# Seven PSUM banks in one list for scores, maxima and all else, and the last sums by products with ones, in a clustered attention with a mixture of experts

## The chip, the core and the metric

One core of one Trainium2 chip runs the whole program. The metric is the device time of one execution in microseconds (us); the time shown for a kernel is the median of its runs. Names of the engines as in the profile: PE is TensorE (PEld its weight loads), DVE is VectorE, ACT is ScalarE, POOL is GpSimd, SP is the engine that issues most of the DMA (SPq in the profile).

## What is computed

A clustered attention, whose output feeds a mixture of experts. Queries and keys are each given to the nearest of 16 centroids of their head, a query sees only the keys of its own cluster, and the rest is softmax attention. The output, 3072 rows of 512, is the input x of the second half: rows with a positive skip score go to one of 8 experts.

```python
# batch, heads, seq, head_dim = 4, 8, 768, 64; 16 clusters
mask = q_assign[:, :, :, None] == k_assign[:, :, None, :]
scores = np.where(mask, scale * np.matmul(q, k.transpose(0, 1, 3, 2)), -1000000000.0)
attn = np.exp(scores - np.max(scores, axis=-1, keepdims=True))
attn = attn / (np.sum(attn, axis=-1, keepdims=True) + 1e-09)
x = attn @ v                                   # 3072 rows of 512
...
e_idx = np.argmax(xc @ w_gate, axis=1)         # for rows with x @ w_skip > 0
h = np.maximum(xc[mask] @ w1[e], 0.0)          # 512 -> 1024, 8 experts
y[mask] = gate_w[mask, None] * (h @ w2[e])     # 1024 -> 512
out[do_compute] = xc + y
```

## The kernel before

**The attention, pair by pair.** The four batches of eight heads make 16 pairs of heads (`npair`; HP = 4 pairs per batch). Scores are kept transposed, keys by queries: one score tile is 128 keys by 384 queries (HALF) of one head. A pair has NS = 24 of them: two halves of the queries (hf), six key tiles (kt), two heads (a). What each step does:

- `smax` (L549, L551): one product of 128 queries by 384 keys, and DVE's maximum over it, 24 per pair. They run for the next pair while the scores of this one run. `mneg` (L557) and `mrows` (L565, L570) turn the maxima into rows that are appended to the operand of the scores.
- `score` (L583, L584, L586): two products into one PSUM bank, and ACT's exp out of it into `PT`, a ring of 12 tiles in SBUF. POOL adds the tiles of the six key tiles up to one sum per half and head (L591, L597); for head 1 of the last pair DVE does.
- `avs` (L608): a group of products of `PT` with v, into the one bank "av", after every third key tile. `oT` keeps its result.
- `sums` (L644, L647), `recip` (L655), `turn_out` (L696) and `xout` with `scale_out` (L701, L718): the row sums by products with ones, their reciprocals, and the output turned and scaled.
- For the pairs to come: `load`, `sims` (L467, L474) and `assign` (L498, with `first_max` behind it) for the clusters, `masks` (L510, L514), and `split_hi` (ACT, L408), `split_lo` (L419, DVE), `copies_hi` (L426) and `copies_lo` (L432), which split q and k in a part of higher and one of lower precision and bring the parts to the operands by DMA on SP. The part of higher precision is kept in `HI[t]` (t = 0 for q, 1 for k), one buffer each for all pairs.

**The order of the work.** Nothing is scheduled by a tool across these steps: `steps` (L297) keeps all of them in a heap by due time and writes instructions in that order. One unit of time is one score; a pair's times count from its first score. The table `PLAN` holds the due times, `FIRST` other ones for the pairs 0, 1 and 2 (each step of them that is not named there takes its time from `PLAN`). A step that yields comes back to the heap at a later time. Every engine takes its instructions strictly in the order in which they were written.

**PSUM.** [...] Before, there are four pools: "ps" with two buffers for the scores, "sm0" to "sm2" for the maxima, "av" with one for the products with v, and "x_ps" with two for all else (clusters, masks, maxima rows, sums, turned outputs, routing). The buffers of a name are used in turn.

**The last pair and the first expert.** `ending` lists what is done with the last pair: sums of its two halves (`sums_last`, L667) and logits, routing of its rows (`gate` with L860 to L877, `route_c`, `route_d` with L922 and L927, `route_e`), and beside it the first expert's work on rows that are known already: `early_first`, `early_turn` and `early_second` take expert 0 through one layer, transposes and the second layer for 128 rows, `second_first` begins the first layer for the next 128 rows (its first half of the hidden columns, 12 products on PE at L986 to L988). `experts` then does the second half of that first layer, the transposes (`turn`, with L996 on PE, L998 on ACT and L999 on DVE), the second layer, and after it the other experts. Weights are read in pieces and split into two parts by ACT (L1229) and DVE (L1230).

Of the kernel before, what the change touches and what calls it, by code (L numbers as in the profile page):

```python
# [12 lines left out]
F32 = mybir.dt.float32  # L13
# [27 lines left out]
NPS = (2, 3, 1, 2)  # L41
# [28 lines left out]
        "load": -62.0, "load_v": -37.0, "assign": (-34.6, 0.25, 0.02, 6.0, 0.02, 0.02), "masks": (-26.0, 0.12), "smax": (-17.6, 0.97, 0.0), "mneg": (-6.4, 5.2),  # L70
# [6 lines left out]
class Kernel:  # L77
# [113 lines left out]
    def attention(self, ctx):  # L191
# [8 lines left out]
        self.st, self.nsm = {}, count()  # L200
# [11 lines left out]
    def centroids(self, cn):  # L212
# [16 lines left out]
        cps = self.xps([P, P])  # L229
# [3 lines left out]
        for t in range(2):  # L233
# [5 lines left out]
            self.cb.append(c)  # L239

# [24 lines left out]
    def keep_busy(self, n, w=4):  # L265

        if not hasattr(self, "idle"):
            self.idle = self.ps_av.tile([P, 512], F32, name="av")
# [101 lines left out]
    def bank(self, name):  # L370
        return (self.ps_st if name == "ps" else self.ps_sm).tile([P, 512], F32, name=name)

    def xps(self, shape):
        return self.ps_x.tile(shape, F32, name="x_ps", tag="x_ps")
# [85 lines left out]
    def sims(self, i):  # L460

        c, nc = self.st[i], self.nc
        sp = self.xps([P, HALF])
# [12 lines left out]
    def first_max(self, vals, n, w, out, tag, pool, wait):  # L476
# [6 lines left out]
        nc.vector.tensor_tensor(out=eq, in0=vals, in1=mx.unsqueeze(2).to_broadcast([P, n, w]), op=ALU.is_ge)  # L483
        yield next(wait)
# [9 lines left out]
    def assign(self, i, *wait):  # L494
        c, nc = self.st[i], self.nc
        tp = self.xps([P, NB, P])
# [6 lines left out]
        yield from self.first_max(tp.rearrange("p b (g c) -> p (b g) c", c=NCL), NB * 8, NCL, oh, "c", self.small, wait)  # L503

    def masks(self, i, wait):

        c, nc = self.st[i], self.nc
        mp = self.xps([P, HALF])
# [5 lines left out]
        nc.scalar.activation(out=mk, in_=mp, func=AF.Identity, scale=self.mscale, bias=self.mbias)  # L514
        yield 0.3
# [19 lines left out]
    def masks_first(self, i):  # L535

        mp = {}
        for t, hf in ((1, 0), (0, 0), (1, 1), (0, 1)):
            mp[t, hf] = self.xps([P, HALF]) if hf == 0 else self.bank("ps")[:, :HALF]
            self.mask_rows(i, t, hf, mp[t, hf])  # L540
        for t, hf, a in ((1, 0, 0), (0, 0, 0), (1, 1, 0), (1, 0, 1), (0, 0, 1), (1, 1, 1), (0, 1, 0), (0, 1, 1)):
            self.mask_out(i, t, hf, a, mp[t, hf])

    def smax(self, i, n):
# [3 lines left out]
        sm = self.bank(f"sm{next(self.nsm) % 3}")[:, :HALF]  # L548
# [896 lines left out]
```

## Time and profile before

| | |
|---|---|
| median of 3 runs | 692.94 us (692.67 to 693.31) |
| the profiled execution's own time | 692.28 us |
| its span, first to last instruction | 690.2 us |
| mean granted clock of TensorE | 0.994 |
| PE / DVE / ACT / POOL busy | 666.2 / 502.4 / 418.4 / 357.7 us |
| DMA | 110.17 MB in 54354 packets, mean 160 GB/s |

The attention fills the span to about 480 us, one pair every 28 us from about 40 us on; the experts follow. In the profile a row of a group names line, engine, operation, the tile that is written and those that are read, the count, the busy time with the mean of one in ns, and the idle time before it with what ended that. "x_ps", "ps", "sm" and "av" are the PSUM tiles, "D" the block that holds the split operands and weights. A group of two numbers like "98*128 98x384" is the size of the weights and of what moves past them. A wait in the list of waits is that of a whole engine, or of its weight loads alone (PEld); "issue" is time in which it waited for nothing that the profile shows. In the timeline a run of equal instructions is one row (x3: three of them).

### The profile page before, as it was taken

Reading aid. Unit: us, or ns where it says so; the run is one execution under the profiler, and the core shown is the slowest. Engines: PE = TensorE matmul, PEld = TensorE weight load, DVE = VectorE, ACT = ScalarE, POOL = GpSimd, SP = SyncE. Lnnn points to the kernel's source line nnn. Section 1 sums busy time; section 2 is a strip of 40 time slices with the busy share of each in tenths; the row PEclk is TensorE's granted clock in tenths of the full one; section 3 lists DMA queues with packets and bytes.
Section 4 is the critical chain, followed back from the end, with each engine's and each line's share of the span. In section 5 each row is a group of like instructions: output and inputs, shape, how many; then the busy total and the mean of one; then the engine's idle time right before and its main releaser. Section 6 shows DMA issues by size and latency. Waiting matters only on the chain.

```text
span 690.2 us, 12370 instructions
## 1 busy us (share of the span) xinstructions
PE 666.2 (97%) x3965; PEld 463.8 (67%) x3965; DVE 502.4 (73%) x1033; ACT 418.4 (61%) x933; POOL 357.7 (52%) x386
## 2 busy tenths in 40 slices
PE   8799999999999999999999999998999999999995
PEld 3565665656666656666666666654688998899783
DVE  7776676768898658898775888987688757665721
ACT  6456676766767676767676676763366455545520
POOL 8765667756668576676775667732213321121101
PEclk9999999999999999999999999999999999999998
DMA  7466656667666663556546544141367658565610
GB/s 207 120 169 168 160 148 163 200 160 209 176 161 180 183 150 113 137 160 177 138 115 154 155 118 119 51 144 55 134 251 230 218 200 274 179 209 199 230 35 31
DMA packets 54354, 110.17 MB, mean 160 GB/s; under 512 B 8615, under 2 KB 22823, under 8 KB 54288
## 3 DMA queue, kind: packets, MB, share of 16 engines
q1 hardware_dynamic: 51232, 101.92, 51.1%
q0 software_dynamic: 2656, 7.24, 3.2%
q8 instruction: 33, 0.54, 0.3%
q14 instruction: 33, 0.27, 0.1%
q10 hardware_dynamic: 400, 0.20, 0.1%
HBM read 61.00 MB, written 10.62 MB: 104 GB/s over the span
## 4 chain that ended last, share of the span: by engine, by line
PE 74%; issue 8%; DMA 8%; DVE 5%; ACT 2%; SPq 1%; POOL 0%; POOLq 0%; DVEq 0%; ACTq 0%
PE av L608 19%; PE ps L583 13%; PE sm L549 10%; PE ps L584 9%; DMA out<-yo,idw 5%; PE ph L988 2%; PE ph L987 2%; PE ph L986 2%; PE x_ps L696 2%; PE py L988 2%; PE py L986 2%; PE py L987 2%; PE x_ps L467 2%; PE x_ps L644 1%; PE x_ps L498 1%
## 5 line engine op out<-in xcount | busy, mean ns | idle before, releaser
L597 POOL TENSOR_TENSOR acc<-acc,PT 128x384 f32<-128x384 f32 x248 | 240.6, 998 | 78.3 <-ACT PT L586 78.0
L551 DVE TENSOR_REDUCE M<-sm 128x1 f32<-128x384 f32 x384 | 202.9, 554 | 72.6 <-PE sm L549 70.2
L586 ACT ACTIVATE PT<-ps 128x384 f32<-128x384 f32 x376 | 182.0, 491 | 111.0 <-PE ps L584 96.3
L583 PE MATMUL ps<-D 98*128 98x384 f32 x376 | 143.1, 380 | 3.6 <-ACT PT L586 2.9
L608 PE MATMUL av<-PT,vt 128*64 128x385 f32 x768 | 139.0, 496 | 0.7 <-ACT PT L586 0.7
L549 PE MATMUL sm<-D 96*128 96x384 f32 x384 | 136.2, 358 | 0.7 <-ACT D L531 0.7
L584 PE MATMUL ps<-D 128*128 128x384 f32 x376 | 127.9, 340 | 0.0
L583 PEld LDWEIGHTS ps<-D 98*128 98x128 f32 x376 | 70.8, 188 | 52.4 <-ACT PT L586 27.6
L591 POOL TENSOR_TENSOR acc<-PT 128x384 f32<-128x384 f32 x64 | 53.9, 862 | 75.7 <-ACT PT L586 45.8
L608 PEld LDWEIGHTS av<-PT,vt 128*64 128x64 f32 x768 | 49.5, 136 | 57.5 <-issue 52.5
L549 PEld LDWEIGHTS sm<-D 96*128 96x128 f32 x384 | 72.9, 190 | 22.6 <-issue 16.2
L1133 POOL DMA_INDIRECT out<-yo,idw x15 | 19.3, 1290 | 116.3 <-DVE yo L1020 105.8
L584 PEld LDWEIGHTS ps<-D 128*128 128x128 f32 x376 | 71.6, 190 | 0.0
L1258 DVE SCALAR_TENSOR_TENSOR hl<-ph,hh 128x256 fp32r<-128x256 f32 x56 | 23.7, 423 | 39.1 <-ACT hh L1257 39.1
L1257 ACT ACTIVATE hh<-ph 128x256 fp32r<-128x256 f32 x56 | 21.4, 382 | 46.9 <-PE ph L988 46.9
L1229 ACT ACTIVATE D<-wraw 128x1024 fp32r<-128x1024 f32 (+1 forms) x45 | 44.1, 1002 | 7.0 <-PE py L988 6.4
L987 PE MATMUL ph<-x2h,D 128*128 128x256 f32 x168 | 47.5, 284 | 0.0
L986 PE MATMUL ph<-x2l,D 128*128 128x256 f32 x168 | 47.5, 283 | 0.0
L986 PE MATMUL py<-D,hh 128*128 128x512 f32 x112 | 45.1, 403 | 0.0
L718 ACT ACTIVATE x<-x_ps,rs 128x64 f32<-128x64 f32 x162 | 36.1, 322 | 9.3 <-DVE rs L660 7.8
L1230 DVE TENSOR_TENSOR D<-wraw,D 128x1024 fp32r<-128x1024 f32 (+1 forms) x29 | 34.4, 1185 | 6.3 <-ACT D L1229 5.6
L987 PE MATMUL py<-D,hh 128*128 128x512 f32 x84 | 32.8, 391 | 0.0
(337 smaller groups left out, 1083.4 us busy)
## 6 DMA issues: line engine op xcount, KB each, us to landing
wraw<-w SPq DMA_DIRECT2D x72, 512.0 KB, 4.6
D<-D SPq DMA_DIRECT2D x124, 192.0 KB, 3.1
raw<-qk SPq DMA_DIRECT2D x16, 768.0 KB, 5.1
D<-raw SPq DMA_DIRECT2D x60, 192.0 KB, 4.1
vt<-v SPq DMA_DIRECT2D x16, 384.0 KB, 4.4
out<-x SPq DMA_DIRECT2D x31, 192.0 KB, 3.4
D<-mk SPq DMA_DIRECT2D x120, 24.0 KB, 1.9
out<-yo,idw POOLq DMA_INDIRECT x15, 4.4
```

The lines of the kernel that those rows point to most:

```text
L549: nc.tensor.matmul(sm, lhsT=c["qm"][a][0:96, j * P:(j + 1) * P], rhs=c["kb"][a][0:96, hf * HALF:(hf + 1) * HALF], start=True, stop=True)
L551: nc.vector.tensor_reduce(out=c["m"][:, j, a, hf:hf + 1], in_=sm, axis=AX.X, op=ALU.max)
L583: nc.tensor.matmul(ps, lhsT=c["kb"][a][0:98, ks], rhs=c["qm"][a][0:98, sl], start=True, stop=False)
L584: nc.tensor.matmul(ps, lhsT=c["kc"][a][:, ks], rhs=c["qc"][a][:, sl], start=False, stop=True)
L586: nc.scalar.activation(out=pt, in_=ps, func=AF.Exp, scale=D ** -0.5)
L591: nc.gpsimd.tensor_tensor(out=acc, in0=self.pt(i, s - 2)[:, :HALF], in1=pt, op=ALU.add)
L597: (nc.vector if dve else nc.gpsimd).tensor_tensor(out=acc, in0=acc, in1=pt, op=ALU.add)
L608: nc.tensor.matmul(av[a * D:(a + 1) * D, :], lhsT=c["vt"][:, kt, a * D:(a + 1) * D], rhs=self.pt(i, hf * 2 * KT + kt * 2 + a), start=(kt = ...
L718: self.nc.scalar.activation(out=c["x"][:, j, cs], in_=xp[:, n, cs], func=AF.Copy, scale=c["rs"][:, j, 2 * hp + a:2 * hp + a + 1])
L986: mm(ps, lhsT=ah, rhs=bl, start=first, stop=False)
L987: mm(ps, lhsT=ah, rhs=bh, start=False, stop=False)
L1229: nc.scalar.activation(out=h[:, cs], in_=r[:, cs], func=AF.Copy)
```

## The change

All eight banks are now tiles of their own, `ps0` to `ps7`. `ps7` is for the products with v (and for the products that keep PE busy at the start). The other seven are in one list: `take` gives the bank that has been free for longest, `give` puts it back at its end, in the order in which the program is written, so that which step gets which bank is fixed when the program is built.

```diff
-        self.ps_st, self.ps_sm = pool("ps_st", NPS[0], space=PSUM), pool("ps_sm", 1, space=PSUM)
-        self.ps_av, self.ps_x = pool("ps_av", NPS[2], space=PSUM), pool("ps_x", NPS[3], space=PSUM)
+        psum = pool("psum", 1, space=PSUM)
+        self.banks = [psum.tile([P, 512], F32, name=f"ps{n}") for n in range(8)]
+        self.free = deque(range(7))
+        self.held = {}
...
+    def take(self, key, shape):
+        b = self.held[key] = self.free.popleft()
+        t = self.banks[b][:, :int(np.prod(shape[1:]))]
...
+    def give(self, key):
+        self.free.append(self.held.pop(key))
...
-        sm = self.bank(f"sm{next(self.nsm) % 3}")[:, :HALF]
+        sm = self.take("sm", [P, HALF])
         nc.tensor.matmul(sm, lhsT=c["qm"][a][0:96, j * P:(j + 1) * P],
                          rhs=c["kb"][a][0:96, hf * HALF:(hf + 1) * HALF], start=True, stop=True)
         nc.vector.tensor_reduce(out=c["m"][:, j, a, hf:hf + 1], in_=sm, axis=AX.X, op=ALU.max)
+        self.give("sm")
...
-        ps = self.bank("sm0" if i == self.npair - 1 and s % 3 == 2 else "ps")[:, :HALF]
+        ps = self.take("ps", [P, HALF])
...
         nc.scalar.activation(out=pt, in_=ps, func=AF.Exp, scale=D ** -0.5)
+        self.give("ps")
...
-            c["av"] = self.ps_av.tile([P, 512], F32, name="av")[:, :HALF + 1]
+            c["av"] = self.banks[7][:, :HALF + 1]
```

Every other user of PSUM in the attention takes and gives in the same way, the bank being given back where its last reader is written.

TensorE's instructions in an ordinary quarter of a pair, behind a group of products with v, are these before (L549 is a maximum's product, L583 and L584 a score's two; the name ahead of the arrow is the PSUM tile, and the number behind its name counts the tiles):

```order
L608 MATMUL av_2885<-PT_65,vt_93 64x385 x6
L549 MATMUL sm2_2971<-D_64 128x384
L583 MATMUL ps_2982<-D_64 128x384
L584 MATMUL ps_2982<-D_64 128x384
L549 MATMUL sm0_2988<-D_64 128x384
L583 MATMUL ps_2992<-D_64 128x384
L584 MATMUL ps_2992<-D_64 128x384
L549 MATMUL sm1_2999<-D_64 128x384
L583 MATMUL ps_3002<-D_64 128x384
L584 MATMUL ps_3002<-D_64 128x384
```

And now (L567 is the maximum's product, L602 and L603 the score's):

```order
L628 MATMUL ps7_88<-PT_65,vt_92 64x385 x6
L567 MATMUL ps3_84<-D_64 128x384
L602 MATMUL ps4_85<-D_64 128x384
L603 MATMUL ps4_85<-D_64 128x384
L567 MATMUL ps6_87<-D_64 128x384
L602 MATMUL ps1_82<-D_64 128x384
L603 MATMUL ps1_82<-D_64 128x384
L567 MATMUL ps2_83<-D_64 128x384
L602 MATMUL ps5_86<-D_64 128x384
L603 MATMUL ps5_86<-D_64 128x384
L567 MATMUL ps0_81<-D_64 128x384
L602 MATMUL ps3_84<-D_64 128x384
```

The instructions stand in the same order; what moved is the bank of each.

**Pair 2's split.** `FIRST[2]` names the times of `split_hi`, `split_lo` and the copies, which it left to `PLAN` before:

```diff
     2: {
-        "load": -62.0, "load_v": -37.0, "assign": (-34.6, 0.25, 0.02, 6.0, 0.02, 0.02), "masks": (-26.0, 0.12), "smax": (-17.6, 0.97, 0.0), "mneg": (-6.4, 5.2),
+        "load": -62.0, "load_v": -37.0, "hi": (-34.25, -28.3), "lo": (-28.35, -22.35), "copies": (-23.3, -23.2, -22.2),
+        "assign": (-34.6, 0.25, 0.02, 6.0, 0.02, 0.02), "masks": (-26.0, 0.12), "smax": (-17.6, 0.97, 0.0), "mneg": (-6.4, 5.2),
```

`PLAN` has `"hi": (-40.35, -34.25)`, `"lo": (-34.35, -28.35)` and `"copies": (-23.3, -23.2, -23.1)`. ACT's instructions during the first pair, from an exp on, before (L408 is `split_hi` of pair 2, first for q and at the end for k; L586 an exp, L570 rows of maxima):

```order
L586 ACTIVATE PT_65<-ps_461 128x384
L408 ACTIVATE D_64<-raw_92 128x768
L586 ACTIVATE PT_65<-ps_483 128x384
L570 ACTIVATE D_64<-x_ps_488 2x384 x2
L586 ACTIVATE PT_65<-ps_497 128x384
L586 ACTIVATE PT_65<-ps_505 128x384
L586 ACTIVATE PT_65<-ps_518 128x384
L586 ACTIVATE PT_65<-ps_527 128x384
L586 ACTIVATE PT_65<-ps_535 128x384
L408 ACTIVATE D_64<-raw_92 128x768
```

And now, from the same exp on (L419 is `split_hi`, L605 an exp, L589 rows of maxima):

```order
L605 ACTIVATE PT_65<-ps0_81 128x384
L605 ACTIVATE PT_65<-ps3_84 128x384
L589 ACTIVATE D_64<-ps4_85 2x384 x2
L605 ACTIVATE PT_65<-ps1_82 128x384
L605 ACTIVATE PT_65<-ps6_87 128x384
L605 ACTIVATE PT_65<-ps3_84 128x384
L605 ACTIVATE PT_65<-ps5_86 128x384
L605 ACTIVATE PT_65<-ps0_81 128x384
L419 ACTIVATE D_64<-raw_91 128x768
```

The cast of q moved behind six more exps and the rows of maxima, to where the cast of k stood; the cast of k moved further back. On SP, the DMAs that `split_hi` issues moved behind loads of v, of wg and of a later pair's q and k.

**The last sums.** For the last pair's second half the sums end with key tile 3 on POOL and DVE; key tiles 4 and 5 are added by PE, by products of `PT` with ones into the bank in which the products of the sums stand. It is done in two parts, at 24.2 and at 25.75.

```diff
-        elif kt > 1:
+        elif kt > 1 and not (i == self.npair - 1 and hf and kt >= KT - 2):
...
-    def sums_last(self, i, hf):
+    def sums_last(self, i, hf, part=0):
...
-        self.last = self.bank("sm1")[:, :HALF]
+        if part == 0:
+            self.last = self.take("last", [P, HALF])
         for a in range(2):
-            self.nc.tensor.matmul(self.last[a * 32:(a + 1) * 32, :], lhsT=self.ones[:, :32], rhs=c[f"acc{hf}{a}"],
-                                  start=True, stop=True)
+            out = self.last[a * 32:(a + 1) * 32, :]
+            if part == 0:
+                self.nc.tensor.matmul(out, lhsT=self.ones[:, :32], rhs=c[f"acc{hf}{a}"], start=True, stop=hf == 0,
+                                      skip_group_check=True)
+            if hf:
+                s = NS - 4 + 2 * part + a
+                self.nc.tensor.matmul(out, lhsT=self.ones[:, :32], rhs=self.pt(i, s)[:, :HALF], start=False,
+                                      stop=part == 1, skip_group_check=True)
...
-        r += [(25.75, self.sums_last, 1), (25.85, self.logits_last, 1, 0.01), (25.9, self.rows_turned, 1),
+        r += [(24.2, self.sums_last, 1, 0), (25.75, self.sums_last, 1, 1), (25.85, self.logits_last, 1, 0.01), (25.9, self.rows_turned, 1),
```

TensorE from the last score's second product on, before (L608 is the last group with v, L667 the sums, L986 the first expert):

```order
L584 MATMUL sm0_5852<-D_64 128x384
L608 MATMUL av_5812<-PT_65,vt0_94 64x385 x6
L667 MATMUL sm1_5884<-acc_5735,ones_109 32x384
L667 MATMUL sm1_5884<-acc_5746,ones_109 32x384
L986 MATMUL sm2_5887<-rawW_5415,xe0_5596 128x512
```

And now (L628 the last group with v; acc_4775 is the sum of head 0, acc_4784 that of head 1):

```order
L603 MATMUL ps1_82<-D_64 128x384
L693 MATMUL ps0_81<-acc_4775,ones_108 32x384
L697 MATMUL ps0_81<-PT_65,ones_108 32x384
L693 MATMUL ps0_81<-acc_4784,ones_108 32x384
L697 MATMUL ps0_81<-PT_65,ones_108 32x384
L628 MATMUL ps7_88<-PT_65,vt0_93 64x385 x6
L697 MATMUL ps0_81<-PT_65,ones_108 32x384 x2
L1026 MATMUL ps2_83<-rawW_4507,xe0_4656 128x512
```

The products with the sums moved from behind the last group with v to ahead of it, and two products with key tile 5 stand behind it.

**The next rows' first layer.** `second_first` now does both halves of the hidden columns, with the transposes of the first half (`early_turn`) within the second; `experts` no longer does them.

```diff
-        r += [(27.0 + k / 100, self.second_first, k) for k in range(KD)]
+        r += [(27.0 + k / 100, self.second_first, k // KD, k % KD) for k in range(2 * KD)]
...
+              (27.055, self.early_turn, 0, at(27.056, 27.19)), (26.45, self.early_second, 2, 4),
...
-        ph = ps_y.tile([P, FF // 2], F32, name="py")
-        for k in range(KD):
-            self.first_layer(self.X1, ph, 1, k)
-            if k == KD // 2 - 1:
-                self.turn(0, bank)
         w1s = split(self.halves[1, 0], "w1", pieces=2)
```

DVE at the end of the attention, before (L851 and L922 prepare the last part of `route_d`, L931 takes its result):

```order
L851 TENSOR_TENSOR rv_5932<-vals_126,ohd_5930 128x3x24
L922 TENSOR_TENSOR rhs3_6078<-rv_5932,hs_5962 128x9x8 x2
L931 TENSOR_TENSOR slotacc_131<-slotacc_131,x_ps_6081 128x48
```

And now (L889, L961 and L970 are the same three; L1096 is `early_turn`'s subtraction):

```order
L889 TENSOR_TENSOR rv_4953<-vals_125,ohd_4951 128x3x24
L1096 TENSOR_TENSOR D_64<-ps2_83,D_64 128x256
L1096 TENSOR_TENSOR D_64<-ps1_82,D_64 128x256
L961 TENSOR_TENSOR rhs3_5109<-rv_4953,hs_4981 128x9x8 x2
L970 TENSOR_TENSOR slotacc_130<-slotacc_130,ps4_85 128x48
```

The two subtractions moved from among the weight splits, where L999 did them, to ahead of rhs. On ACT, the second relu and the copies of these transposes moved ahead of all eight splits of the next expert's weights.

More of the change, by code (lines that the diff above doesn't have):

```diff
@@ L2 @@
 import heapq
+from collections import deque
 from contextlib import ExitStack
@@ L40 @@
 OT = 64
-NPS = (2, 3, 1, 2)
 RING = 8
@@ L267, in keep_busy @@
         if not hasattr(self, "idle"):
-            self.idle = self.ps_av.tile([P, 512], F32, name="av")
+            self.idle = self.banks[7]
         for _ in range(n):
@@ L368, in tasks @@
         return r
[L370 to L374, printed above, removed]
+    def take(self, key, shape):
+        b = self.held[key] = self.free.popleft()
+        t = self.banks[b][:, :int(np.prod(shape[1:]))]
+        if len(shape) == 2:
+            return t
+        dims = "abcd"[:len(shape) - 1]
+        return t.rearrange(f"p ({' '.join(dims)}) -> p {' '.join(dims)}", **dict(zip(dims[1:], shape[2:])))
+    def give(self, key):
+        self.free.append(self.held.pop(key))
     def load(self, i):
@@ L474, in sims, with first_max @@
             nc.scalar.activation(out=c["ss"], in_=sp, func=AF.Copy)
-    def first_max(self, vals, n, w, out, tag, pool, wait):
+        self.give("sims")
+    def first_max(self, vals, n, w, out, tag, pool, wait, key=None):
         nc = self.nc
@@ L538, in masks_first @@
         for t, hf in ((1, 0), (0, 0), (1, 1), (0, 1)):
-            mp[t, hf] = self.xps([P, HALF]) if hf == 0 else self.bank("ps")[:, :HALF]
+            mp[t, hf] = self.take((t, hf), [P, HALF])
             self.mask_rows(i, t, hf, mp[t, hf])
@@ L640, in sums @@
         c, nc = self.st[i], self.nc
-        sp = self.xps([P, HALF])
+        sp = self.take("sums", [P, HALF])
         w = P // (2 * len(hfs))
@@ L647, in sums @@
         nc.scalar.activation(out=c["sr"], in_=sp, func=AF.Copy, bias=GUARD)
+        self.give("sums")
         c["hfs"] = hfs
@@ L680, in logits_last @@
                                     op0=ALU.add)
+        self.give("last")
     def rows_turned(self, i, hf):
         c, nc = self.st[i], self.nc
-        tp = self.xps([P, NB, P])[:, :, :96]
+        tp = self.take("rows", [P, NB, P])[:, :, :96]
         for b in range(NB):
@@ L809, in part_last @@
         nc, small, R, bt = self.nc, self.rt, 32 * (HP - 1), i // HP
-        tp = self.xps([P, NB, R])
+        tp = self.take("part", [P, NB, R])
         for b in range(NB):
@@ L1023, in early_first, with second_first @@
         if k == 0:
-            self.ph = self.bank("ps" if c else "sm2")
+            self.ph = self.take("ph", [P, 512])
         self.first_layer(self.xes, self.ph, c, k)
-    def second_first(self, i, k):
+        if k == KD - 1:
+            self.give("ph")
+    def second_first(self, i, c, k):
         if k == 0:
-            self.ph = self.bank("sm1")
-        self.first_layer(self.X1, self.ph, 0, k)
+            self.ph = self.take("ph", [P, 512])
+        self.first_layer(self.X1, self.ph, c, k)
+        if k == KD - 1:
+            self.give("ph")
     def early_bank(self):
-        self.nbank = getattr(self, "nbank", 0) + 1
-        return self.bank(f"sm{self.nbank % 2}")[:, :CT * P]
+        t = self.take("turn", [P, CT * P])
+        self.give("turn")
+        return t
     def early_turn(self, i, c, wait):
@@ L1052, in early_turn @@
                                     in1=h.rearrange("p f t -> p (f t)").bitcast(F32), op=ALU.subtract)
+        for f in fs[::CT]:
+            self.give(("turn", f))
     def early_second(self, i, a, b):
         if a == 0:
-            self.py = self.bank("sm2")
+            self.py = self.take("py", [P, 512])
         for f in range(a, b):
```

57 lines of the change are left out of this document (39 added, 18 removed).

## The prediction

> **What bounds the kernel now.** I read the page first. TensorE is busy nearly from end to end, and the clock row dips only in the third slice and the last.
>
> ```profile
> span 690.2 us, 12370 instructions
> ...
> PE 666.2 (97%) x3965; PEld 463.8 (67%) x3965; DVE 502.4 (73%) x1033; ACT 418.4 (61%) x933; POOL 357.7 (52%) x386
> ...
> PE   8799999999999999999999999998999999999995
> ...
> PEclk9999999999999999999999999999999999999998
> ```
>
> The page's 97% for PE hides a loss, because a product whose predecessor has not yet run out is drawn with its end overlapping. So next come the waits of the weight loads (PEld) in the attention stage, 41.5 to 455 us. Columns: total us, times, longest.
>
> ```profile
> PEld ps L583 <- ACT PT L586: 23.5, 92, 0.5
> ...
> PEld ps L583 <- ACT x L718: 7.2, 12, 0.6
> ...
> PEld x_ps L498 <- ACT sr L647: 3.7, 9, 0.4
> ...
> PEld sm L549 <- DVE M L551: 2.4, 5, 0.6
> PEld av L608 <- ACT PT L586: 2.4, 14, 0.2
> ```
>
> A score's first product (L583) waits 92 + 12 = 104 times for ScalarE: the exp (L586) two scores earlier must have read the bank, since scores rotate through two. Maxima (L549), with three banks, wait for VectorE 5 times only. What one such wait costs PE is read from a piece of its timeline (start, duration):
>
> ```profile
> 240.47 0.34 PE L549 MATMUL sm<-D 96*128 96x384 f32 x1
> 240.65 0.34 PE L583 MATMUL ps<-D 98*128 98x384 f32 x1
> 240.82 0.34 PE L584 MATMUL ps<-D 128*128 128x384 f32 x1
> 241.00 0.33 PE L549 MATMUL sm<-D 96*128 96x384 f32 x1
> 241.27 0.45 PE L583 MATMUL ps<-D 98*128 98x384 f32 x1
> 241.55 0.34 PE L584 MATMUL ps<-D 128*128 128x384 f32 x1
> 241.73 0.34 PE L549 MATMUL sm<-D 96*128 96x384 f32 x1
> ```
>
> Undisturbed products start 0.175 us apart (240.47 to 241.00 is three steps). The product at 241.27 waited: it starts 0.27 after its predecessor and the next one 0.28 after it, so 0.095 + 0.105 = 0.20 us are lost per wait. How much room the other engines have, by stretches (PE, PEld, DVE, ACT, POOL busy with counts; then clock, DMA share, GB/s): one whole pair with the densest VectorE, then the start, then the place where the experts begin.
>
> ```profile
> 179.00:207.00 28.00, 27.82 (x167) 17.84 (x166) 26.08 (x54) 19.80 (x49) 18.52 (x20) 1.00 0.68 186
> ...
> 36.00:41.20 5.20, 5.20 (x23) 2.85 (x22) 3.65 (x6) 2.20 (x4) 2.62 (x4) 0.67 1.00 206
> ...
> 510.00:530.00 20.00, 20.00 (x136) 18.34 (x136) 14.87 (x25) 9.23 (x18) 7.17 (x6) 1.00 0.84 280
> ```
>
> ScalarE (19.80 of 28) and GpSimd (18.52) have room; VectorE has 1.9 us of 28 in this pair. One maximum and one exp take (last mean, ns):
>
> ```profile
> L551 DVE TENSOR_REDUCE M<-sm 128x1 f32<-128x384 f32 x384 | 202.9, 554 | 72.6 <-PE sm L549 70.2
> L586 ACT ACTIVATE PT<-ps 128x384 f32<-128x384 f32 x376 | 182.0, 491 | 111.0 <-PE ps L584 96.3
> ```
>
> **The change, part by part.**
>
> *Seven banks in one list.* A score's bank is now asked for again five to seven takes later instead of at the second next score. In the quarter shown with the change, ps3 goes from the maximum at its head to the score ten rows further: ten products x 0.175 = 1.75 us from the start of the one to that of the other, of which the product (0.33) and the maximum (0.55) need 0.88; an exp needs 0.49. So I let the waits go: 104 x 0.20 = 20.8 us, of which I take 20. The ends are 92 x 0.20 = 18.4 (the twelve behind the turn-outs' scaling, L718, stay) and 20.8. What is late next: a score and a maximum are three products, 3 x 0.175 = 0.53 us, in which ScalarE does one exp of 0.49, so it keeps up between the groups with v (L608) and catches up during them. Those groups, whose one bank stays, wait for their exps 14 times already (2.4 us together as loads); if ScalarE falls behind, that row grows first.
>
> *The other PSUM users.* assign (L498) behind the sums' copy waits 9 times in the row above (3.7 us as loads wait, of which PE idles less), because x_ps too had two banks; the routing's second half does the same. 12 such places x 0.2 = 2.4 us; the bounds are 1.2 (half of them wait for data, not for the bank) and 3.7 (the row as it stands). I take 2.4.
>
> *The densest pairs.* A pair that shortens from 28.0 to 28.0 - 1.5 = 26.5 us (20 + 2.4 over 15 pairs) still holds VectorE's 26.08. But then VectorE is 98% busy, and three pairs are of this kind (the routing of batches 0 to 2 falls into the pairs that follow them). Nothing in the trace shows PE against such a VectorE; from 0 to 0.5 us each, I put +0.5 in all (0 to +1.5).
>
> *The start.* Pair 2's cast of q and k (split_hi, L408) leaves its place between ScalarE's exps.
>
> ```profile
> 28.86 2.52 SPq L426 DMA_DIRECT2D D<-D  x4
> ...
> 32.69 0.84 ACT L408 ACTIVATE D<-raw 128x768 fp32r<-128x768 f32 x1 [4.35 <-DMA D<-D]
> ...
> 33.96 0.45 PE L583 MATMUL ps<-D 98*128 98x384 f32 x1 [2.12 <-ACT PT L586]
> ...
> 35.36 0.45 PE L583 MATMUL ps<-D 98*128 98x384 f32 x1 [0.60 <-ACT PT L586]
> ...
> 36.37 0.52 PE L549 MATMUL sm<-D 96*128 96x384 f32 x1
> ...
> 38.46 2.77 PE L608 MATMUL av<-PT,vt 128*64 128x385 f32 x12
> 41.16 0.44 PE L583 MATMUL ps<-D 98*128 98x384 f32 x1
> ```
>
> The cast overwrites a buffer from which pair 1's copies (L426) are still being read, so ScalarE stands 4.35 us in front of it, the exps queue behind, and PE idles 2.12 + 0.60 us. In the new order it stands six exps and the rows of maxima further on. It began to wait at 32.69 - 4.35 = 28.34; six scores with their maxima (0.53 each) and one group with v (2.1) later is 33.6, after the copies have landed. So 2.72 us go. Right after these idles, the granted clock in 36.00 to 41.20 is 0.67: products take 0.52 where 0.34 is usual, and the group with v 2.77. If the clock stays at full speed, 5.20 x (1 - 0.67) = 1.7 us go too. Together 4.4; without the clock part 2.7. [...] What moves with it: the two casts' DMAs on SP come behind loads of v and wg, and pair 2's first maxima, which need them, stand 10 scores and more later in the table, over 10 us; so nothing else is late.
>
> *The last sums.* The order before: VectorE's last add, then two products. Now part 0 stands ahead of the last group with v, and needs the add that stands at 474.57:
>
> ```profile
> 474.57 0.55 DVE L597 TENSOR_TENSOR acc<-acc,PT 128x384 f32<-128x384 f32 x1
> ...
> 473.40 2.16 PE L608 MATMUL av<-PT,vt 128*64 128x385 f32 x12 [0.65 <-ACT PT L586]
> 475.49 0.83 PE L667 MATMUL sm<-acc,ones 128*32 128x384 f32 x2
> 477.68 0.83 PE L667 MATMUL sm<-acc,ones 128*32 128x384 f32 x2 [1.36 <-DVE acc L597]
> 478.44 0.50 PE L986 MATMUL sm<-rawW,xe 128*128 128x512 f32 x1
> ```
>
> Before, PE waits 0.65 and 1.36. Now the adds of the last two key tiles are replaced by four products, but PE waits until 474.57 + 0.55 = 475.1 with the group behind it. One product with ones is two instructions and takes 0.76 (477.68 to 478.44). So part 0's second head ends at 475.1 + 2 x 0.76 = 476.6, the group takes 2.09 (473.40 to 475.49) and part 1 at most 1.52: the expert's product starts at 480.2 if the two heads of part 1 follow one another, at 479.5 if they overlap as those of the group with v do (twelve in 2.09), against 478.44. That is +1.1 to +1.8. Were the add early and part 0's heads to overlap as well, it would be 473.40 - 0.65 + 1.52 + 2.09 + 0.76 = 477.1, that is -1.3. I take +1.2.
>
> *The second half of the next expert's first layer, with its transposes, moved ahead of the experts.*
>
> ```profile
> 497.80 0.38 DVE L922 TENSOR_TENSOR rhs<-rv,hs 128x72 bf16<-128x72 bf16 x2
> ...
> 505.42 0.75 DVE L999 TENSOR_TENSOR D<-tp,D 128x256 fp32r<-128x256 f32 x2
> ...
> 498.23 0.23 PE L927 MATMUL x_ps<-rhs,oht 128*128 128x48 bf16 x3 [0.70 <-DVE rhs L922]
> ...
> 499.53 0.39 PE L988 MATMUL py<-D 128*128 128x512 f32 x1
> 499.76 0.60 PE L996 MATMUL tp<-ident,PT 128*128 128x128 f32 x4
> 500.11 0.48 PE L986 MATMUL py<-D 128*128 128x512 f32 x1
> ...
> 505.90 0.50 PE L988 MATMUL py<-D 128*128 128x512 f32 x1 [0.24 <-DVE D L999]
> ```
>
> The 12 products fill PE's idle 0.70, a gain of 0.7. But VectorE's two subtractions of the transposes (0.75) now stand ahead of rhs. Those need half of the 12 products (6 x 0.23, 499.53 to 499.76, from about 497.4: 498.8), the transposes (0.35, 499.76 to 500.11) and a copy on ScalarE, which the nearest row, one such subtraction (0.75 / 2), prices at 0.38: 499.5. With the 0.75 and rhs's 0.38 the latter is done near 500.6 instead of 498.2, and all that VectorE does behind it, the eight weight splits (L1230) among them, is 2.4 late. The second pair of subtractions (505.42) stands behind those splits; less the 0.75 already done, it starts at 505.42 + 2.4 - 0.75 = 507.1. PE, which waited 0.24 for it before and went on at 505.90, 0.48 behind its start, goes on at 507.6: 1.7 later. From 510 on it has 20.00 of 20 busy, so nothing is made up. I take +1.7, between -0.7 (the splits keep up after all) and +3.0 (ScalarE's splits, which now stand behind the second relu as well, are late by that much).
>
> **The sum.** -20 - 2.4 + 0.5 - 4.4 + 1.2 + 1.7 = -23.4 us. The profiled execution took 692.28 us (span 690.2 and 2.1 around it), 0.66 under the median of 692.94. 692.28 - 23.4 + 0.66 = 669.5 us.
>
> **The rivals.**
> - *Other engines catch PE (half the gain).* The wait of the score moves to the exp, the maximum or the add behind it: for it speaks VectorE's 26.08 of 28, against it that most pairs leave more (ScalarE 8.2 and GpSimd 9.5 us per pair even here). With 11 of the 22.4 us: 669.5 + 11.4 = 681. Chance 0.10.
> - *The stall at the start stays*, because another transfer is late there: 669.5 + 4.4 = 674. For it, a DMA share of 1.00 in that stretch. Chance 0.06.
> - *The end costs more*, 3.0 us in the experts, 1.8 in the sums and 1.5 in the dense pairs, the upper bounds together: 669.5 + 1.3 + 0.6 + 1.0 = 672.4. Chance 0.10.
> - *The banks are not the cause*: the score waits for ScalarE's pace and the list only renames the wait. Then the start and the end alone count: 692.94 - 4.4 + 1.2 + 1.7 = 691.4; with the start's clock still low 693.1. Against it: ScalarE has 8 us idle per pair. Chance 0.04, half of it no change.
> - *Slower: VectorE's maxima now hold up the scores.* With one list, a score takes a bank that a maximum gave back; before, a late maximum held up a maximum only. Where VectorE trails PE by over 1.75 - 0.88 = 0.9 us, each of the 48 scores and maxima of a pair may wait, 48 x 0.20 = 9.6 us instead of 104 / 15 x 0.20 = 1.4. It decides once it holds in more than three pairs: four cost 4 x 8.2 = 33, and 669.5 + 33 = 702. Against it: 5 waits of maxima in 413 us. Chance 0.03.
> - *PE rests more often, so the clock falls.* The start's row shows full speed lost (0.67 over 5.20 us) after short idles; a clock of 0.67 over one such stretch in each of the 16 pairs would cost 16 x 1.7 = 27 us: 669.5 + 27 = 696. The trace shows 1.00 in the long windows, with a wait every 4 us. Chance 0.01. [...]
>
> **How the numbers follow.** The forecast case has 0.66; its own range is from 663 (the good bounds of the banks and the end together, 669.5 - 0.8 - 1.3 - 2.5 - 2.4 = 662.5) to 674 (the bad ones of them, 669.5 + 1.6 + 1.2 + 1.9 = 674.2). Upward, 678 takes in the rivals of the start and the end and a part of the first; left out are most of the first, the three last and a little below 663, about 2 in 10. About 0.2% (1.4 us) is what a measurement can tell here. Faster: 0.66 + 0.10 + 0.06 + 0.10 + 0.02 = 0.94; the same: 0.02; slower: 0.03 + 0.01 = 0.04.
>
> **What would show it.** In the new profile the row "ps, exp" among the weight loads' waits should fall from 104 to a handful, and the pairs shorten from 28.0 to about 26.5 us, while VectorE's share rises over 0.9. The 2.12 and 0.60 are gone and the clock at 36 to 41 us is 1.00. PE waits 2 to 3 us before the last group with v, none behind it, and about 3 us in the first expert's second layer. Wrong it is if scores wait for maxima as often as they did for exps, if the pairs keep their length, or if the stage after 481 us shortens.

## The result, and the profile after

The changed kernel takes 667.71 us (median of 4 runs, 666.52 to 669.92), the kernel before 692.81 beside it; the ratio is 0.964, 95% interval 0.9619 to 0.9662. The forecast was 669.5. The profiled execution is the slowest of the four: 669.92 us, span 668.1.

The page, as before: span, busy engines, and the clock in 40 slices.

```profile
span 668.1 us, 12396 instructions
...
PE 644.7 (96%) x3973; PEld 476.9 (71%) x3973; DVE 505.4 (76%) x1031; ACT 418.3 (63%) x933; POOL 357.3 (53%) x384
...
PEclk9999999999999999999999999799999999999998
```

TensorE's busy time fell by 21.5 us though it has 8 instructions more: most of what the waits cost before was counted as busy. The other engines' busy times are within 3 us of those before. The waits of the weight loads in the attention (32 to 432 us; a score's first product is now L602):

```profile
PEld ps L602 <- issue: 17.3, 28, 1.1
...
PEld ps L602 <- DVE M L569: 4.1, 1, 4.1
```

The row of 92 waits for the exp is gone; what is left on L602 waited for nothing in particular, with one exception of 4.1 us, to which we come. From the second group with v to the last but five (38.46 to 441.13 before, 33.72 to 409.97 after), both with 2330 products:

```profile
38.46:441.13 402.67, 398.69 (x2330) 253.12 (x2329) 312.49 (x635) 279.76 (x679) 267.88 (x285) 1.00 0.57 155
```

```profile
33.72:409.97 376.25, 373.79 (x2330) 263.06 (x2329) 314.12 (x635) 280.69 (x680) 271.17 (x287) 1.00 0.63 168
```

26.4 us less for the same products, at the same clock of 1.00. Now the start, TensorE and ScalarE of the changed kernel:

```profile
33.72 2.16 PE L628 MATMUL ps<-PT,vt 128*64 128x385 f32 x12
35.81 0.44 PE L602 MATMUL ps<-D 98*128 98x384 f32 x1
```

```profile
33.76 0.84 ACT L419 ACTIVATE D<-raw 128x768 fp32r<-128x768 f32 x1
```

The cast finds its buffer free (no idle time stands at the end of its row), and the group that took 2.77 us at 38.46 takes 2.16 at 33.72. That is 4.7 us up to here.

**One place gives some of it back.** TensorE in the second half of the pair before the last; then VectorE; then GpSimd; all of the changed kernel:

```profile
409.97 2.16 PE L628 MATMUL ps<-PT,vt 128*64 128x385 f32 x12
...
414.11 0.33 PE L567 MATMUL ps<-D 96*128 96x384 f32 x1
418.20 0.69 PE L602 MATMUL ps<-D 98*128 98x384 f32 x1 [3.76 <-DVE M L569]
418.69 0.52 PE L603 MATMUL ps<-D 128*128 128x384 f32 x1
...
421.06 4.03 PE L628 MATMUL ps<-PT,vt 128*64 128x385 f32 x12
```

```profile
410.43 6.70 DVE L1202 TENSOR_TENSOR gatee<-slotacc 128x1 f32<-128x1 f32 x1
```

```profile
409.95 7.17 POOL L617 TENSOR_TENSOR acc<-acc,PT 128x384 f32<-128x384 f32 x8
```

A sum of one element per partition lies on VectorE for 6.70 us (the next one of that size, L1203 at 417.17, takes 0.16) and ends with GpSimd's row of eight adds (409.95 + 7.17 = 417.12). Behind it stand five maxima with their banks; once the list is used up, the next score stands still for 3.76 us, and the products after it run at 0.52 instead of 0.34, the next group with v at 4.03 instead of 2.16. In the kernel before the same sum was held too, with GpSimd's row of four adds, and no product waited for it:

```profile
441.38 2.74 DVE L1151 TENSOR_TENSOR gatee<-slotacc 128x1 f32<-128x1 f32 x1
```

```profile
440.50 3.60 POOL L597 TENSOR_TENSOR acc<-acc,PT 128x384 f32<-128x384 f32 x4
444.57 3.62 POOL L597 TENSOR_TENSOR acc<-acc,PT 128x384 f32<-128x384 f32 x4 [0.47 <-ACT PT L586]
```

There GpSimd ran out of exps for 0.47 us after the fourth add, and the sum came free; now the exps are ahead of it and the row is eight adds long.

**The end.** The last sums on TensorE, and VectorE's part of them:

```profile
449.27 0.83 PE L693 MATMUL ps<-acc,ones 128*32 128x384 f32 x2
...
450.68 2.16 PE L628 MATMUL ps<-PT,vt 128*64 128x385 f32 x12
452.77 0.84 PE L697 MATMUL ps<-PT,ones 128*32 128x384 f32 x4
453.54 0.50 PE L1026 MATMUL ps<-rawW,xe 128*128 128x512 f32 x1
```

```profile
447.70 0.16 DVE L915 TENSOR_TENSOR g<-g,vals 128x3 f32<-128x3 f32 x1
...
448.66 0.55 DVE L617 TENSOR_TENSOR acc<-acc,PT 128x384 f32<-128x384 f32 x1
```

No wait stands in TensorE's rows: VectorE's add ends at 449.2, just when head 1's product needs it. And the next rows' first layer:

```profile
475.02 0.37 DVE L961 TENSOR_TENSOR rhs<-rv,hs 128x72 bf16<-128x72 bf16 x2
...
481.97 0.75 DVE L1039 TENSOR_TENSOR D<-tp,D 128x256 fp32r<-128x256 f32 x2
```

```profile
480.62 0.50 PE L1026 MATMUL py<-D 128*128 128x512 f32 x1 [0.72 <-ACT D L1038]
...
482.44 0.50 PE L1028 MATMUL py<-D 128*128 128x512 f32 x1 [1.09 <-DVE D L1039]
...
487.13 0.27 PE L1026 MATMUL ph<-x2l,D 128*128 128x256 f32 x1
```

TensorE waits for the second pair of subtractions as forecast. From the first expert's first product (453.54, before 478.44) to expert 1's hidden layer (487.13, before 508.99) it is 33.6 us, before 30.5.

### The profile page after: what moved, and what is told of

Its sections match the earlier page's. It is cut to its first block, busy times and chain, and to the rows that moved or that the text cites. A ratio compares the mean times of both kernels' runs of the same rounds, so it can differ in the third digit from the quotient of the medians.

```text
span 668.1 us, 12396 instructions
## 1 busy us (share of the span) xinstructions
PE 644.7 (96%) x3973; PEld 476.9 (71%) x3973; DVE 505.4 (76%) x1031; ACT 418.3 (63%) x933; POOL 357.3 (53%) x384
## 4 chain that ended last, share of the span: by engine, by line
PE 71%; DMA 10%; issue 9%; DVE 9%; POOL 0%; ACT 0%; POOLq 0%; DVEq 0%
PE ps L628 19%; PE ps L602 10%; PE ps L567 10%; PE ps L603 9%; DMA out<-yo,idw 6%; DVE M L569 3%; PE ps L727 2%; DMA xg<-out,idr 2%; PE ph L1028 2%; PE ph L1027 2%; PE ph L1026 2%; PE ps L584 2%; PE ps L478 1%; PE py L1028 1%; PE py L1026 1%
## 5 line engine op out<-in xcount | busy, mean ns | idle before, releaser
L605 ACT ACTIVATE PT<-ps 128x384 f32<-128x384 f32 x384 | 184.5, 492 | 95.4 <-PE ps L603 78.4
L569 DVE TENSOR_REDUCE M<-ps 128x1 f32<-128x384 f32 x384 | 200.2, 554 | 46.1 <-PE ps L567 45.1
L628 PE MATMUL ps<-PT,vt 128*64 128x385 f32 x768 | 140.2, 500 | 0.0
L602 PE MATMUL ps<-D 98*128 98x384 f32 x384 | 135.1, 352 | 4.3 <-DVE M L569 3.8
L567 PE MATMUL ps<-D 96*128 96x384 f32 x384 | 134.9, 358 | 0.9 <-ACT D L547 0.7
L603 PE MATMUL ps<-D 128*128 128x384 f32 x384 | 130.4, 340 | 0.0
L602 PEld LDWEIGHTS ps<-D 98*128 98x128 f32 x384 | 73.1, 190 | 25.3 <-issue 19.1
L628 PEld LDWEIGHTS ps<-PT,vt 128*64 128x64 f32 x768 | 49.8, 137 | 57.8 <-issue 53.1
L567 PEld LDWEIGHTS ps<-D 96*128 96x128 f32 x384 | 73.0, 191 | 21.3 <-issue 7.2
L603 PEld LDWEIGHTS ps<-D 128*128 128x128 f32 x384 | 73.3, 191 | 0.0
L1308 ACT ACTIVATE hh<-ph 128x256 fp32r<-128x256 f32 x56 | 21.5, 383 | 46.8 <-PE ph L1028 45.8
L1026 PE MATMUL py<-D,hh 128*128 128x512 f32 x112 | 45.1, 402 | 0.0
L749 ACT ACTIVATE x<-ps,rs 128x64 f32<-128x64 f32 x162 | 36.2, 322 | 10.2 <-DVE rs L681 9.1
L429 DVE TENSOR_TENSOR raw<-raw,D 128x768 fp32r<-128x768 f32 x28 | 39.2, 1401 | 0.0
```

Of the source, the lines that this page charges most:

```text
L429: eng.tensor_tensor(out=lo.bitcast(F32R), in0=lo, in1=c[f"hi{t}"].bitcast(F32), op=ALU.subtract)
L567: nc.tensor.matmul(sm, lhsT=c["qm"][a][0:96, j * P:(j + 1) * P], rhs=c["kb"][a][0:96, hf * HALF:(hf + 1) * HALF], start=True, stop=True)
L569: nc.vector.tensor_reduce(out=c["m"][:, j, a, hf:hf + 1], in_=sm, axis=AX.X, op=ALU.max)
L602: nc.tensor.matmul(ps, lhsT=c["kb"][a][0:98, ks], rhs=c["qm"][a][0:98, sl], start=True, stop=False)
L603: nc.tensor.matmul(ps, lhsT=c["kc"][a][:, ks], rhs=c["qc"][a][:, sl], start=False, stop=True)
L605: nc.scalar.activation(out=pt, in_=ps, func=AF.Exp, scale=D ** -0.5)
```

## The experiments

Twelve kernels, in three groups, each with runs of the kernel before (692.8 to 693.2) beside it. Times are medians; ratios are to the kernel before.

**e0, the changed kernel again.** 

> The changed kernel once more, to stand beside the three below on the same chip. Expected 667.7 us (its first four runs gave 666.5 to 669.9). Theory H (VectorE's tiny sum L1202 is held until GpSimd's run of adds ends, so five maxima wait behind it and the score takes none of their banks): the wait of PE of about 3.8 us near 418 us is there again, and L1202 ends within 0.1 us of the end of an add on GpSimd. Rival V (VectorE was late there by its own load, in one execution): the wait is under 1 us or lies elsewhere.

668.3 us (664.78 to 669.76). The sum was held again, for 6.70 us (411.45 to 418.16), GpSimd's eighth add ending at 418.14. So it is no chance of one execution. The runs scatter over 5 us, those of the kernel before over less than 2.

**e1, the banks dealt as before.** `take` draws from three lists instead of one (the ending's first layers, transposes and last sums from that of the maxima).

```diff
-        self.free = deque(range(7))
+        self.free = {"ps": deque((0, 1)), "sm": deque((2, 3, 4)), "x": deque((5, 6))}
```

> The changed kernel with its seven banks dealt as before: two in turn for the scores, three for the maxima, two for all else; the other three edits stay. Theory B (the list ends 104 waits of scores for their bank): most of the gain is gone, 692.8 - 4.9 (start) + about 2 (end) = 690, and the weight loads' waits of scores for the exp are back near 100 in the attention. Rival S (the gain is from the start and the rest): 670 to 675.

697.63 us, ratio 1.0062 (1.0045 to 1.0079): the gain is gone, and more. Its weight loads in the attention wait as before:

```profile
PEld ps L607 <- ACT PT L610: 23.2, 91, 0.4
...
PEld ps L607 <- ACT x L754: 7.2, 12, 0.6
PEld ps L681 <- DVE eqc L500: 6.8, 12, 0.6
```

91 + 12 waits of scores are back, so theory B holds. It is 7.6 us above the 690 expected, in three places. The start gains 1.1 us here and not 4.9: the second group with v stands at 37.40, but the first already at 30.26, 2.9 later than in the changed kernel; half of that may be the clock, which is 0.50 from 16.3 to 19.6 (an estimate: 3.3 us at half speed lose 1.7). The stretch of the attention up to the sum is 3.1 us longer than before, and there the last row above is new: the turned outputs wait for the clusters' maxima, 12 times. A likely reason, not tried by itself, is that "all else" here gets the bank given back first and not every second one. And the next rows' first layer, which stays moved, costs 3.4 where about 2 was expected.

**e2, pair 2's split at its old times** (the line of `FIRST[2]` as before). 

> The changed kernel with pair 2's split at the times of before. The forecast's step (cast in front of the copies' landing, 2.7 us of PE idle and 1.7 of clock): 4.4 us slower than the changed kernel, 672.1; by the shift of the second group with v in the profile (0.5 to 4.75 us ahead) 4.2, 671.9. Rival (seven banks let the exps fall behind without stopping PE): 668 to 669.

671.43 us (670.07 to 672.18), 3.1 to 3.7 above the changed kernel's two medians. ScalarE and TensorE of e2:

```profile
33.64 0.84 ACT L419 ACTIVATE D<-raw 128x768 fp32r<-128x768 f32 x1 [4.77 <-DMA D<-D]
```

```profile
34.91 0.44 PE L602 MATMUL ps<-D 98*128 98x384 f32 x1 [2.02 <-ACT PT L605]
...
37.55 2.16 PE L628 MATMUL ps<-PT,vt 128*64 128x385 f32 x12
```

```profile
35.00:41.00 6.00, 5.74 (x32) 3.86 (x33) 4.55 (x7) 4.08 (x10) 4.43 (x6) 1.00 1.02 233
```

The cast waits again (4.77), TensorE too (2.02). The second group stands at 37.55 instead of 33.72, 3.8 later. But 1.05 of this is not the split's: e2's first group with v already stands at 28.44 instead of 27.39, while in e6, which has the old split too, it stands at 27.37. From the first group to the second it is 9.11 us in e2 and 9.09 in e6, against 6.33 in the changed kernel: 2.8 more, the forecast's 2.7 of idle. Seven banks do not cover it, so that part of the step is real. The forecast's other part, 1.7 for the clock, did not come back: behind the wait the clock is 1.00 in e2 (the row of the window above, third figure from its end), and in e6 as well (34 to 43), where the kernel before had 0.67.

**e3, the last sums as before** (adds of key tiles 4 and 5 on GpSimd and VectorE, the products behind the last group with v). 

> The changed kernel with the last sums of the kernel before: all adds on GpSimd and VectorE, the products with ones behind the last group with v. The forecast's step (the new order costs 1.2 us): 1.2 us faster than the changed kernel, 666.5. The theory after the profile (the gate's operations on VectorE are held less, as GpSimd has two adds less, so the add came in time and the step costs nothing): 0 to 1.3 us slower, 667.7 to 669.0, with VectorE's operations L912 and L915 of 0.7 to 1 us again between the last adds, and PE waiting about 1.4 us for the last add.

666.94 us (665.08 to 668.05) against 668.3 (664.78 to 669.76): in time the two can't be told apart. The trace can, VectorE and TensorE of e3:

```profile
446.14 0.96 DVE L909 TENSOR_TENSOR g<-g,vals 128x3 f32<-128x3 f32 x1
```

```profile
451.55 0.83 PE L692 MATMUL ps<-acc,ones 128*32 128x384 f32 x2 [1.49 <-DVE acc L617]
```

The operation of three elements that takes 0.16 in the changed kernel takes 0.96 here, with GpSimd's two adds still running, and TensorE waits 1.49 for the last add. From the last pair's third group with v to the first expert's first product it is 9.89 us in e3 and 9.88 in e6, which has the old order too, 9.95 before; in the changed kernel and e0 it is 9.56. So the new order gains about 0.35 us.

**e4, the next rows' second half back in the experts** (the block of `experts` as before, `second_first` with one half). 

> The changed kernel with the second half of the next rows' first layer, its transposes and its relu back in the experts. The forecast's step (they cost 1.7 us, as the weight splits start late): 666.0, 1.7 us faster than the changed kernel; the profile of the changed kernel would make it up to 3 us (hidden layer of expert 1 starts 21.9 us earlier than before, where the first expert's first product is 24.9 us earlier). Rival (the loss is the lower clock at 482 to 486 us of that one execution, and the 0.7 of the wait that the products fill is a gain): 0.7 us slower, 668.4.

666.26 us (662.43 to 666.93), ratio 0.96 (0.9576 to 0.9623); e0's is 0.9629 (0.9603 to 0.9655), so in time the intervals overlap. From the first expert's first product to expert 1's hidden layer: 30.33 us, as before (30.54); in e0 31.98. That is 1.65 us for the move, the forecast's 1.7. The changed kernel's own trace had 33.6, and the difference is the clock, by windows around that place of the changed kernel and of e0 (the third figure from the end is the clock):

```profile
474.00:487.20 13.20, 10.87 (x47) 8.12 (x46) 11.63 (x32) 9.93 (x20) 0.00 (x0) 0.87 0.48 170
```

```profile
473.00:486.00 13.00, 10.67 (x57) 8.09 (x56) 11.14 (x32) 10.23 (x22) 0.40 (x1) 1.00 0.41 129
```

Of the ten profiles with the move in place, four show 31.8 to 32.0 (e0, e3, e5, e13) and six 33.3 to 34.0; the four without it (before, e4, e6, e9) all show 30.2 to 30.5.

**e5, the tiny sums on GpSimd.**

```diff
-        nc.vector.tensor_tensor(out=g, in0=acc[:, 3, :], in1=acc[:, 4, :], op=ALU.add)
-        nc.vector.tensor_tensor(out=g, in0=acc[:, 2, :], in1=g, op=ALU.add)
+        eng = self.nc.gpsimd if tag == "e" else self.nc.vector
+        eng.tensor_tensor(out=g, in0=acc[:, 3, :], in1=acc[:, 4, :], op=ALU.add)
+        eng.tensor_tensor(out=g, in0=acc[:, 2, :], in1=g, op=ALU.add)
```

> The changed kernel with the two tiny sums of the early rows' gates (L1202, L1203, 128x1) on GpSimd instead of VectorE; nothing else. Theory H: the wait of 3.76 us for a maximum at 418 us and the low clock behind it (0.52 for 0.34 over some seven products, 1.1 us) go: 663 to 664, 3.8 to 4.9 us faster than the changed kernel. Rival V: within 0.5 us of the changed kernel, and a wait for a maximum stays at that place.

661.48 us (661.2 to 662.84), ratio 0.9554 (0.954 to 0.9567): 6.8 below e0, more than the 3.8 to 4.9 of the wait and the clock behind it. The group at 409.96 is followed by the next at 415.96, 6.0 us later, where the changed kernel has 11.1; and the next stretch falls from 10.35 to 8.46. This second part is the clock: behind the wait it is 0.50 for 6.7 us in the changed kernel (first row), and the next group with v, 4.03 there, takes 2.16 in e5 (second row).

```profile
418.10:424.80 6.70, 6.60 (x21) 3.67 (x21) 4.79 (x14) 2.87 (x4) 0.00 (x0) 0.50 0.18 42
```

```profile
415.96 2.16 PE L628 MATMUL ps<-PT,vt 128*64 128x385 f32 x12
```

So of the 7.0 us some 3.4 are the clock (an estimate: half of 6.7), where 1.1 were expected. VectorE and GpSimd of e5:

```profile
410.42 3.20 DVE L987 TENSOR_TENSOR cc<-ohd,ecode 128x48 f32<-128x48 bf16 x1
```

```profile
409.93 3.61 POOL L617 TENSOR_TENSOR acc<-acc,PT 128x384 f32<-128x384 f32 x4
413.50 0.18 POOL L1202 TENSOR_TENSOR gatee<-slotacc 128x1 f32<-128x1 f32 x1
413.77 0.19 POOL L1203 TENSOR_TENSOR gatee<-slotacc,gatee 128x1 f32<-128x1 f32 x1
```

Now the operation behind the sums is held, but for 3.20 us, up to GpSimd's first sum; the seven banks cover that, and no product waits. So it is not the sum alone: the operation that now stands in its place is held too.

**e12, the sums as one reduction on VectorE.**

```diff
+        if tag == "e":
+            nc.vector.tensor_reduce(out=g, in_=acc[:, 2:5, :].rearrange("p v s -> p s v"), axis=AX.X, op=ALU.add)
+            return g
```

> The changed kernel with the two tiny sums on VectorE as one reduction of 128x3 to 128x1. Theory H: the reduction, which has one input, takes 0.2 us, but the operation behind it (two inputs) is held in its place for some 6 us: 667 to 668.5, no gain. Rival F (L1202 alone is held, because of its strided inputs): 661.5.

668.03 us (666.48 to 669.65), no gain. VectorE of e12:

```profile
410.43 0.15 DVE L1203 TENSOR_REDUCE gatee<-slotacc 128x1 f32<-128x3 f32 x1
410.49 6.69 DVE L987 TENSOR_TENSOR cc<-ohd,ecode 128x48 f32<-128x48 bf16 x1
```

The reduction, with one input from SBUF, passes at once; the next operation with two inputs is held in its place for 6.69 us. Rival F falls.

**e13, a tiny sum between GpSimd's adds.**

```diff
+            if i == self.npair - 2 and hf:
+                tiny = self.small.tile([P, 1], F32, name="tiny")
+                nc.gpsimd.tensor_tensor(out=tiny, in0=self.ident[:, :1], in1=self.ident[:, 1:2], op=ALU.add)
```

> The changed kernel, with a tiny sum of 128x1 on GpSimd behind each of the eight adds of the second half of the pair before the last (it computes nothing that is used); the sum L1202 stays on VectorE. Theory H (VectorE's operation with two inputs from SBUF is held for as long as GpSimd's adds follow one another without a gap; in e5 the next such operation was held 3.20 us and came free when GpSimd reached the two tiny sums): held 1 us at most, PE's wait of 3.8 us gone, 661.5 to 662.5. Rival (the gain of e5 came from taking the two sums off VectorE): 667 to 668.5.

668.53 us (668.02 to 670.72): no gain, so theory H fails in the form in which it was put there. VectorE, and the first and the last of GpSimd's rows, of e13:

```profile
410.56 7.70 DVE L1205 TENSOR_TENSOR gatee<-slotacc 128x1 f32<-128x1 f32 x1
```

```profile
411.04 0.18 POOL L620 TENSOR_TENSOR tiny<-ident 128x1 f32<-128x1 f32 x1
...
417.26 0.98 POOL L617 TENSOR_TENSOR acc<-acc,PT 128x384 f32<-128x384 f32 x1
```

The tiny sums free nothing; the sum is held to the end of the row (418.26), over seven adds and the tiny sums between them. So a short instruction among the adds (0.18) did not free it here. What freed the operation in e5 is not shown. GpSimd does stand idle there, for 0.09 us, because its second sum needs the first; but that gap begins at 413.68 (413.50 + 0.18), and the held operation had ended at 413.62 (410.42 + 3.20), 0.08 behind the fourth add. In e6 the sum came free after three adds with a fourth following at once, and the next two operations with two inputs were held for one add each (0.93 and 0.94). What decides when a held operation gets its turn stays open.

**e6, the list alone** (start, sums and next rows as before). 

> The kernel before with the list of banks alone: start, last sums and the next rows' first layer as before. Theory B: 692.8 - 26.4 (gain from the second group with v to the pair before the last, by the profile) + 4 to 5 (the wait behind the held sum) = 670 to 671; by the forecast's sum 692.9 - 21.9 = 671.0. Rival S: 685 or more.

669.49 us (665.91 to 673.08), ratio 0.9678 (0.9645 to 0.971). Rival S falls: the list alone is nearly the whole gain. Here the sum is held for 3.15 us only in the profiled execution, and the runs scatter over 7 us.

**e7, five banks in the list** (`range(5)`). 

> The changed kernel with five banks in the list instead of seven; the other two stay unused. If only the depth over the exp counts (ten products of 0.175 us between a bank's two uses with seven, about seven with five, 1.2 us, where a product and a maximum need 0.9): within 3 us of the changed kernel, 668 to 671. If VectorE's lag behind PE is often over 0.3 us: 675 to 690, with scores waiting for maxima in most pairs.

679.24 us (678.02 to 680.5), ratio 0.9796 (0.9776 to 0.9816). Its weight loads:

```profile
PEld ps L602 <- DVE eqc L495: 11.4, 12, 1.3
...
PEld ps L602 <- DVE M L569: 5.5, 11, 1.0
```

The time lies in the second range of the expectation, whose condition, waits for maxima in most pairs, is there in part (11 in 15 pairs). The larger row is another one, which was not expected: the banks that a step holds for long. `first_max` keeps one for several units, and with five the scores come to it 12 times.

**e8, as e5 with two lists**, three banks for the maxima, four for all else. 

> As e5 (tiny sums on GpSimd), but the seven banks in two lists: three for the maxima, four for the scores and all else. If depth for the scores is what counts: 661.5 to 663, as e5. If it counts that any step may take any bank: the banks that the clusters' maxima (first_max) hold for some ticks are then missing to the scores, 12 waits of up to 1 us as with five banks: 665 to 675.

670.48 us (669.02 to 670.72), 9 above e5. Its attention, from the second group with v to the one behind the held operation, is 5.5 us longer, with the turned outputs waiting for the clusters' maxima:

```profile
PEld ps L681 <- DVE eqc L500: 7.6, 12, 1.0
```

Another 1.6 lie in the next rows' first layer, which took 33.4 here (one of the six above) and 31.8 in e5. So in this division it counts that any step may take any bank, beside the depth; other divisions were not tried.

**e9, e4 and e5 together.** 

> The changed kernel with the tiny sums on GpSimd (e5) and the next rows' first layer's second half in the experts (e4): 661.5 - 2.0 = 659.5; by the profiles of e4 and e5 661.5 - 1.6 = 659.9. If the two gains overlap: 661 to 662.

659.78 us (659.64 to 660.08), ratio 0.9514 (0.9501 to 0.9527), faster than both kernels and as expected. Its runs lie within 0.5 us.

## Why the prediction was right, step by step

The time came out 1.8 us under the forecast, within its range; but that is in part luck, for terms that were off in both directions make up that sum. In the order of the sum, measured against the profile of before:

| step | forecast | measured | from |
|---|---|---|---|
| scores' waits for the bank | -20 | -20.5 | all 696 starts of score products, second group with v to the last pair, before against e5 |
| other users of PSUM | -2.4 | -6.1 | the rest of that stretch (408.9 to 382.3); 4.7 of it the clusters' transposes |
| densest pairs | +0.5 | 0 | 179 to 205, below |
| start | -4.4 | -4.7 | second group with v, 38.46 to 33.72; 2.8 of it idle, by e2 and e6 |
| held operation | not in the sum | +7.0 | 5.1 + 1.9, groups at 409.97 to 431.41 against e5; some 3.4 of it the clock |
| last sums | +1.2 | -0.4 | 9.95 to 9.56 |
| next rows' first layer | +1.7 | +1.5 (clock full), +3.1 (low) | 30.5 to 32.0 and to 33.6 |

The measured terms add up to -23.2 us with the clock full in the next rows' first layer and to -21.6 with it low. The profiled executions are 22.4 apart (692.28 and 669.92), the medians 25.1.

- *Scores.* The mechanism and the price of 0.20 per wait were right: e1 brings the waits back and takes the gain, and over all starts the 92 waits for the exp cost 0.20 each, 18.4 in all, the forecast's lower end. The count of 104 was not. The 12 waits behind the scaling (L718) gained nothing: their scores stand right behind a group with v, where the two starts take 0.34 us longer in e5 too. The rest of the 20.5 comes from ten waits that the forecast left out, 0.14 each, and from small delays of the others. So the 20 were met in part by luck. The row left out, of the kernel before:

```profile
PEld ps L583 <- ACT vm L628: 1.9, 10, 0.2
```

- *Other users.* The step was mis-sized: 12 places at 0.20 each. The assign rows alone give 4.7 / 12 = 0.39 each; why twice the price of a score's wait was not tried.
- *Densest pairs.* No engine caught TensorE. The pair of the routing, changed kernel:

```profile
179.00:205.00 26.00, 25.68 (x162) 17.92 (x161) 23.87 (x48) 19.16 (x48) 18.69 (x20) 1.00 0.72 192
```

VectorE has 23.87 of 26.0 us in that stretch, and the pairs in the middle of the attention are 25.7 to 27.7 us apart.
- *The rival in which maxima hold up the scores* was given 0.03 for more than three pairs. It came true in one place and cost 7.0 us there. What was missing in the prediction is the cause: it weighed VectorE by its load, and the delay comes from GpSimd. It looked at VectorE's waits, and a held operation is no wait in the profile but a long row. The row was there to be read before (L1151, 2.74 us for one element); without the list no product waited for it, with the list it is what stops TensorE for 3.76 us.
- *Last sums.* The step that failed is "PE waits until 474.57 + 0.55 = 475.1": the add came earlier, because the two adds less on GpSimd shortened the gate's operations ahead of it (0.96 and 0.70 before, 0.16 after; e3 brings 0.96 back). A chain on VectorE was taken as fixed though the change touched the engine that holds it up.
- *Next rows.* Right in mechanism and size. The low clock behind it, in six of ten profiles, was not foreseen.
- *The clock.* Its loss at the start was priced and is gone; but e2 and e6 have the idle back and the full clock (1.00) there, so this gain hangs on the execution. And the clock falls at places that the prediction did not price. At the held sum it falls in all eight profiles with seven banks in one list and that wait (to 0.50 over 418.1 to 424.8 in the changed kernel), for some 6.8 us in some (the changed kernel, e0, e13) and 3.4 in others (e3, e6, e12). Near 482 us it falls in six of ten (0.74 over 480.6 to 487.2 in the changed kernel), and in e0 and e4 it is 0.50 from 21.3 to 24.6 as well. This is the greater part of what spreads the runs. The mean granted clock of each run is on record: in e0 0.989 for the slowest run (669.76) and 0.994 for the fastest (664.78), and 0.005 of 667 us is 3.3 of these 5.0 us (an estimate). It is not all: in e6 two runs with 0.993 took 665.91 and 668.18. The runs of e9, which has neither of the two waits, lie within 0.5 us and have 0.995 to 0.997.

## What to carry to other kernels

A wait of 0.2 us that occurs a hundred times hides in a "97% busy" row; count the waits of the weight loads and price one from the timeline. When the pools of PSUM become one list, look for every step that holds a bank long, and for every instruction of an engine whose row is ten times its usual length: with the private buffers gone, such a row of 6.70 us stopped TensorE for 3.76 here. After such a change profile again at the place with the longest single wait; here moving two instructions of 0.2 us to another engine gave 6.8 us.

## What the runs showed of the hardware

In these traces an operation on VectorE with two inputs from SBUF stood still while GpSimd ran adds one behind the other: 2.74 us over three adds before, 6.70 over seven after, 7.70 in e13 over seven adds and the tiny sums between them, each time ending within 0.03 us of the end of an add and without a turn between the adds before it. It did not always last to the end of the row: 3.15 us over three adds in e6, with a fourth following. With two adds taken off GpSimd an operation of 0.96 us took 0.16, and with them put back 0.96 again (e3). A reduction with one input in the same place took 0.15 (e12).

TensorE's clock fell after a single wait of 3.76 us (products of 0.52 instead of 0.34 from 418.69 on), and in some executions after waits of 0.72 and 1.09 close together (0.87 over 474 to 487), in others not (1.00 in e0). Behind a wait of 2.02 us in e2 it stayed at 1.00 (35 to 41), where in the kernel before, behind 2.12 and 0.60, it was 0.67.
